# Taking VectorE's and GpSimd's SBUF-to-SBUF operations one at a time in the planner of a delta-rule and two-expert-layer kernel

## The chip, the cores and the metric

The kernel runs on one core of a Trainium2 chip. Its time is device microseconds of one execution; the figure for the kernel before is the median of three runs. A core has the engines TensorE (PE in the profile), VectorE (DVE), ScalarE (ACT) and GpSimd (POOL), each with its own in-order queue of instructions, and SyncE (SP), which here issues the DMA transfers.

## The reference

Three stages follow one another, all in float32. `q`, `k`, `v` are 4 x 8 x 768 x 48 (batch, heads, steps, head size):

```python
k_n = k / (np.linalg.norm(k, axis=-1, keepdims=True) + 1e-06)
for t in range(S):                       # S = 768
    y[:, :, t] = np.einsum('bhd,bhde->bhe', q[:, :, t], state)
    v_old = np.einsum('bhde,bhd->bhe', state, kt)
    state = state + bt * np.einsum('bhd,bhe->bhde', kt, vt - v_old)
...
# first expert layer, x is 3072 x 384, w_in 384 x 2048, w_out 2048 x 384
h = x @ w_in
P = a[0] + a[1] * h + a[2] * h2 + a[3] * h3
Q = 1.0 + np.abs(b[0]) * np.abs(h) + np.abs(b[1]) * h2
x = (P / (Q + 1e-06)) @ w_out
# second expert layer
r = np.maximum(x @ w_in, 0.0)
out = (r * r) @ w_out
```

## The kernel before

**Attention.** The 768 steps are cut into blocks; six groups, g = 0 to 5, each prepare 128 rows of small triangular systems. For a group a Gram matrix `Gb` (128 x 1024) is formed from `k`, scaled (L519 to L534), and a unit triangular matrix is inverted into `Tt` by 31 elimination steps of two instructions each: a product `tmp<-Gb,Tt` (L546) and a subtraction `Tt<-Tt,tmp` (L550), 128 x 31 up to 128 x 256 elements. Group 0's 62 instructions stand on VectorE, those of groups 1 to 5 on GpSimd. `vn` (128 x 768, the values by chunk) is scaled by L678. The products of the attention are PE's matmuls of L735; VectorE masks some of their results with `tri` (L780).

**Expert layers.** The 3072 tokens are six tiles of 512 columns (i = 0 to 5); the 2048 hidden features are sixteen blocks of 128 (j = 0 to 15). h(i,j) is the first product of a block, nine matmuls of L1031: weights `A` against the tile's high and low halves `xh` and `xl`. The rational function is a chain over PSUM and SBUF tiles: `a` (L1054), `b` (L1056 and L1066), `c` (L1058 to L1068), `h` and `g` (L1069 to L1071). Then `g` is cut in a high half `ph` (ScalarE, L1088) and a low half `pl` (GpSimd or VectorE, L1089), and acc(j), nine matmuls of L1118, adds the block to three accumulators from `ph`, `pl` and the weights `E` and `F` (L1115 with the unsplit weights `B` in the first tiles). Layer 2 has the same form with relu squared: `b`, `gh`, `gl` (L1132 to L1136) and L1145 to L1147 on weights `C`.

**Weights.** A block's input and output weights arrive packed, 128 x 768, in a staging buffer (`raw`, `rb`, `ra`, `mem`), are unpacked by ScalarE (L962) and VectorE (L964, L973 to L983), and are then split into halves: the high one by a ScalarE copy (L990, L997), the low one by a subtraction (L991 for `A`, L998 for `C`), on GpSimd or VectorE for `A` and on GpSimd for `C`. raw(l,j) is the load for layer l, block j. The loads of layer 2's first blocks alternate between two buffers `raw2_0` and `raw2_1`; a buffer can be loaded again when the `A` and the `C` split that read it are done. `rb0`, `rb1`, ... are further staging buffers.

**What sets the order.** All work is entered as tasks of a planner, class `Plan`: engine, planned duration, what is read and written, a due time. `play()` is a list scheduler: it holds a time at which each engine comes free, starts the task that can start first and, among those within 0.15 us, the one due first, and advances the engine by the planned duration. `run()` does eight rounds of it, moves the due times back from the uses in between, and keeps the best order. That order is then emitted, so that planned durations fix in which order instructions stand on each queue; on the chip each queue runs as data and semaphores allow. Tasks made by `shared` may go to GpSimd or VectorE, those made by `either` to ScalarE or VectorE; `play()` picks the engine. Each task carries a flag `lock`, set for operations whose operands lie in SBUF on VectorE and GpSimd, which `play()` does not read in the kernel before. A planned duration there is an average that includes some waiting, for example this one, with `SLOW` = 1.08:

```python
add(eng, (0.17 + 2.3e-3 * a * b) * (SLOW if g == 1 else 1) if g else 0.19 + 1.04e-3 * a * b, st, ...)
```

## Time and profile before

| | kernel before |
|---|---|
| median of 3 runs (lowest, highest) | 1009.11 us (1009.02, 1010.25) |
| the profiled execution's own time | 1008.75 us |
| its span, first to last instruction | 1007.0 us |
| PE busy | 958.9 us (95% of the span) |
| DVE, ACT, POOL busy | 686.4, 617.3, 510.0 us |
| mean granted TensorE clock | 0.97 |

The profiled execution lies 0.36 us under the median and has 1.75 us outside the span. A page shows busy time by engine; a table of windows shows it by stretch of the span; a list of waits names, for one engine, who it waited for; a timeline has the instructions of an engine in order of time with the idle time before each in brackets.

### The profile page before, as it was taken

The page shows a single profiled execution, that of the slowest core. Times are in us where ns is not written, and L with a number is a line of the kernel's source. Part 1 is how long each engine was busy: PE and PEld are TensorE (multiplying, and loading weights), DVE is VectorE, ACT ScalarE, POOL GpSimd, SP SyncE. Part 2 cuts the span into 40 slices and gives each one's busy share as a digit, 9 for nine tenths or more (in the row PEclk, how much of TensorE's full clock was granted, in tenths as well). Part 3 has the DMA queues.
Part 4 walks back from the last instruction along what each step waited for, and adds up shares of the span by engine and source line. Part 5 has one row for each costly group of instructions (what it writes and reads, how often), then busy time and mean ns, then how long its engine had stood idle before and what let it go on. Part 6 is the DMA issues. An engine that isn't in the chain of part 4 may idle for free.

```text
span 1007.0 us, 23528 instructions
## 1 busy us (share of the span) xinstructions
PE 958.9 (95%) x9611; PEld 770.5 (77%) x9611; DVE 686.4 (68%) x1100; ACT 617.3 (61%) x1121; POOL 510.0 (51%) x625
## 2 busy tenths in 40 slices
PE   5487999999999999999999999999999999999998
PEld 5485665688778878878888877888888888888886
DVE  6968988987987798789779999953343433434332
ACT  4668677888878697678779776743332333423322
POOL 3188998988998989875448986710000000000000
...
GB/s 160 253 223 128 142 212 206 83 54 131 64 109 96 140 89 43 84 109 46 34 68 63 36 122 261 115 53 11 1 63 1 32 32 0 32 1 1 32 1 31
DMA packets 126668, 84.66 MB, mean 84 GB/s; under 512 B 95584, under 2 KB 111520, under 8 KB 126560
## 3 DMA queue, kind: packets, MB, share of 16 engines
...
## 4 chain that ended last, share of the span: by engine, by line
PE 72%; POOL 15%; DVE 3%; ACT 3%; issue 3%; SPq 2%; DMA 1%; POOLq 0%; ACTq 0%; DVEq 0%
PE bank L1031 31%; PE bank L1118 11%; PE bank L735 7%; PE bank L1147 7%; PE bank L1145 7%; PE bank L1146 7%; POOL Tt L550 3%; POOL pl L1089 3%; POOL tmp L546 3%; POOL mem L1066 3%; SPq L357 2%; PE bank L638 1%; POOL A L991 1%; PE bank L1115 1%; PE bank L624 1%
## 5 line engine op out<-in xcount | busy, mean ns | idle before, releaser
L1031 PE MATMUL bank<-xh,A 128*128 128x512 f32 (+1 forms) x1170 | 301.5, 393 | 3.4 <-POOL A L991 3.1
L1031 PEld LDWEIGHTS bank<-xh,A 128*128 128x128 f32 x1170 | 217.6, 189 | 56.6 <-POOL A L991 6.7
L1133 DVE SCALAR_TENSOR_TENSOR mem<-bank,mem 128x512 f32<-128x512 f32 x96 | 66.2, 689 | 145.9 <-ACT mem L1132 145.9
L1031 PE MATMUL bank<-xl,A 128*128 128x512 f32 (+1 forms) x585 | 163.3, 388 | 0.0
L1132 ACT ACTIVATE mem<-bank 128x512 f32<-128x512 f32 x96 | 57.4, 598 | 147.3 <-PE bank L1031 145.5
L1066 POOL TENSOR_TENSOR mem<-mem 128x512 f32<-128x512 f32 x89 | 117.0, 1315 | 51.0 <-ACT mem L1058 46.7
L1031 PEld LDWEIGHTS bank<-xl,A 128*128 128x128 f32 x585 | 109.8, 189 | 22.6
L1089 POOL TENSOR_TENSOR pl<-mem,ph 128x512 fp32r<-128x512 f32 x80 | 106.4, 1330 | 22.4 <-ACT ph L1088 22.3
L1136 DVE TENSOR_TENSOR gl<-mem,gh 128x512 fp32r<-128x512 f32 x96 | 71.7, 747 | 63.3 <-ACT gh L1135 63.2
L1147 PE MATMUL bank<-gh,C 128*128 128x512 f32 x288 | 113.8, 395 | 0.0
L1145 PE MATMUL bank<-gl,C 128*128 128x512 f32 x288 | 113.6, 394 | 0.0
L1146 PE MATMUL bank<-gh,C 128*128 128x512 f32 x288 | 112.0, 389 | 0.0
L1135 ACT CAST gh<-mem 128x512 fp32r<-128x512 f32 x96 | 59.6, 621 | 78.2 <-DVE mem L1133 66.2
L1118 PE MATMUL bank<-pl,E 128*128 128x512 f32 x240 | 98.9, 412 | 6.9 <-POOL pl L1089 6.9
L550 POOL TENSOR_TENSOR Tt<-Tt,tmp 128x31 f32<-128x31 f32 (+15 forms) x155 | 93.0, 600 | 8.1
L1118 PE MATMUL bank<-ph,E 128*128 128x512 f32 x240 | 94.2, 393 | 0.0
L1118 PE MATMUL bank<-ph,F 128*128 128x512 f32 x240 | 94.2, 393 | 0.0
L546 POOL TENSOR_TENSOR tmp<-Gb,Tt 128x31 f32<-128x31 f32 (+15 forms) x155 | 86.8, 560 | 9.3
L1069 DVE SCALAR_TENSOR_TENSOR mem<-mem,par,bank 128x512 f32<-128x512 f32 x96 | 71.3, 743 | 29.4 <-ACT bank L1079 28.3
L1078 ACT ACTIVATE mem<-mem,par 128x512 f32<-128x512 f32 x96 | 69.4, 723 | 25.0 <-POOL mem L1066 23.6
L1054 ACT ACTIVATE mem<-bank 128x512 f32<-128x512 f32 x96 | 56.9, 593 | 42.3 <-PE bank L1031 32.7
L1067 DVE TENSOR_TENSOR mem<-bank,mem 128x512 f32<-128x512 f32 x96 | 65.7, 684 | 12.0 <-ACT mem L372 11.4
...
## 6 DMA issues: line engine op xcount, KB each, us to landing
raw<-in_w_dram SPq DMA_DIRECT2D x17, 768.0 KB, 4.8
rb<-in_w_dram SPq DMA_DIRECT2D x8, 768.0 KB, 5.0
...
```

The lines of the kernel that those rows point to most:

```text
L546: E_.tensor_tensor(tv, _mid(Gb[:, s, s + 1:32], [128, a, b]), Tt[:, 0:a, s:s + 1].to_broadcast([128, a, b]), op=ALU.mult)
L550: E_.tensor_tensor(Tt[:, 0:a, s + 1:32], Tt[:, 0:a, s + 1:32], tv, op=ALU.subtract)
L735: M.matmul(*y[:3], start=a, stop=z)
L1031: M.matmul(h, a, b, start=(m == 0), stop=(m == len(seq) - 1))
L1066: shared(1.32, 0.75, lambda E: E.tensor_tensor(b(), b(), a(), op=ALU.mult), r=[ak], w=[bk], due=due + 4.2)
L1069: q3 = lambda: V.scalar_tensor_tensor(c(), c(), s(0), h(), op0=ALU.add, op1=ALU.mult)
L1089: shared(1.3, 0.72, lambda E: E.tensor_tensor(slot[mk][0], g(), slot[pk][0], op=ALU.subtract), r=[gk, pk], w=[mk], due=due + 11.5, alloc=( ...
L1118: M.matmul(acc[d], a, b, start=(j == 0 and m == 0), stop=(j == NJ - 1 and m == 2))
L1136: add("DVE", 0.76, lambda: V.tensor_tensor(gl(), b(), gh(), op=ALU.subtract), r=[bk, gk, "late"], w=[lk], due=due + 5, lock=1, alloc=(("gl ...
L1145: M.matmul(acc[d], wh, gl, start=(j == 0), stop=False)
L1146: M.matmul(acc[d], wl, gh, start=False, stop=False)
L1147: M.matmul(acc[d], wh, gh, start=False, stop=(j == NJ - 1))
```

## The change

`play()` gets a second clock, `port`. A task with `lock` on VectorE or GpSimd may only start when `port` has passed, and sets it to its own end less 0.12 us, so that in the plan such operations of the two engines follow one another. The planned durations of these tasks become those that the operation has without another one beside it. `shared` gets an argument `free_port` that clears the flag; it is used for the scaling of `vn`. The tasks r1 and r2 lose the flag, the product `b` of the first blocks gains it. Nothing is computed in another way: what changes on the chip is the order of instructions on the queues, some buffers, and the engine of some alternates (five operations go from VectorE to GpSimd, among them a split of `A0` and layer 2's split of `A2`; two go from GpSimd to VectorE, one chunk of `vn` and pl(2,13)). Below L235 every line number of the changed kernel is 5 higher (L546 is L551, L550 is L555, L678 is L683, L991 is L996, L998 is L1003, L1031 is L1036, L1089 is L1094, L1118 is L1123).

```diff
-SLOW = 1.08
+PORT = ("DVE", "POOL")
...
             s = max(when[i], free_at[e])
+            if e in PORT and (t["alt"][e][2] if t["alt"] else t["lock"]):
+                s = max(s, port)
...
+        port = 0.0
         while True:
...
                 free_at[e] = end if e != "LAND" else 0.0
+                if e in PORT and t["lock"]:
+                    port = end - 0.12
...
-    def shared(dur, dve, f, **kw):
+    def shared(dur, dve, f, free_port=False, **kw):
 
-        return add(("POOL", "DVE"), (dur, dve), (lambda: f(P_), lambda: f(V)), lock=(1, 1), **kw)
+        return add(("POOL", "DVE"), (dur, dve), (lambda: f(P_), lambda: f(V)), lock=(0, 0) if free_port else (1, 1), **kw)
...
-                add(eng, (0.17 + 2.3e-3 * a * b) * (SLOW if g == 1 else 1) if g else 0.19 + 1.04e-3 * a * b, st, r=GB, w=[tt, tm_], due=d1, lock=1)
+                add(eng, 0.22 + 1.72e-3 * a * b if g else 0.19 + 1.04e-3 * a * b, st, r=GB, w=[tt, tm_], due=d1, lock=1)
...
-                    shared(1.55, 1.4, vs, r=[("nT", g % 2)], w=[("vn", cb, x) for x in range(B)], due=dn - 4)
+                    shared(1.5, 1.2, vs, free_port=True, r=[("nT", g % 2)], w=[("vn", cb, x) for x in range(B)], due=dn - 4)
...
-        shared(1.15, LOW, lambda E: E.tensor_tensor(Aw[j][:, so], af(), Aw[j][:, si], op=ALU.subtract),
+        shared(1.02, 0.54, lambda E: E.tensor_tensor(Aw[j][:, so], af(), Aw[j][:, si], op=ALU.subtract),
...
-            shared(1.32, 0.75, lambda E: E.tensor_tensor(b(), b(), a(), op=ALU.mult), r=[ak], w=[bk], due=due + 4.2)
+            shared(1.29, 0.7, lambda E: E.tensor_tensor(b(), b(), a(), op=ALU.mult), r=[ak], w=[bk], due=due + 4.2)
```

The other edits of the diff are of this last kind: a number for a planned duration (L973 1.05 to 0.95, L977 0.7 to 0.55, L979 0.84 to 0.66, L964 0.95 to 0.58, L983 1.15 to 0.95, L998 1.15 to 1.02, L1015 0.75 to 0.7, L1136 0.76 to 0.7).

**Place 1, GpSimd, end of group 1's elimination.** `Gb_129` and `Tt_131` are group 1's matrices, `Gb_128` and `Tt_130` group 2's; `A_88` is layer 1's split weight A4, which h(0,4) needs; `vn_144` and `vn_145` are two chunks of the values. Before, with the last elimination steps:

```order
L550 TENSOR_TENSOR Tt_131<-Tt_131,tmp_133 128x31
L991 TENSOR_TENSOR A_88<-B_179,A_88 128x384
L678 TENSOR_TENSOR vn_144<-vn_144,nT_140 128x768
L678 TENSOR_TENSOR vn_145<-vn_145,nT_140 128x768
L991 TENSOR_TENSOR A_89<-B_179,A_89 128x384
L546 TENSOR_TENSOR tmp_132<-Gb_128,Tt_130 128x31
```

After, some twenty rows earlier:

```order
L551 TENSOR_TENSOR tmp_133<-Gb_129,Tt_131 128x175
L683 TENSOR_TENSOR vn_145<-vn_145,nT_140 128x768
L555 TENSOR_TENSOR Tt_131<-Tt_131,tmp_133 128x25x7
L551 TENSOR_TENSOR tmp_133<-Gb_129,Tt_131 128x156
L555 TENSOR_TENSOR Tt_131<-Tt_131,tmp_133 128x26x6
```

and after, at the end of the elimination:

```order
L551 TENSOR_TENSOR tmp_133<-Gb_129,Tt_131 128x31
L555 TENSOR_TENSOR Tt_131<-Tt_131,tmp_133 128x31
L996 TENSOR_TENSOR A_88<-B_179,A_88 128x384
L996 TENSOR_TENSOR A_91<-ra_1079,A_91 128x384
L551 TENSOR_TENSOR tmp_132<-Gb_128,Tt_130 128x31
```

One chunk of `vn` now stands ahead of A4 and the other has left this queue; a split of A0 (`A_84<-mem,A_84`) also stands in the elimination now, some thirty rows ahead of A4.

**Place 2, VectorE and GpSimd, near the end of layer 1.** VectorE before, in the chain of block (5,12), whose tile is `bank4`; `raw2_0` holds layer 2's raw weights of blocks 1 and 3 in turn:

```order
L1067 TENSOR_TENSOR mem_102<-bank4_73,mem_102 128x512
L1068 SCALAR_TENSOR_TENSOR mem_102<-mem_102,par_82,bank4_73 128x512
L964 TENSOR_SCALAR raw2_0_7003<-raw2_0_7003 128x768
L991 TENSOR_TENSOR A2_86<-raw2_1_7004,A2_86 128x384
L1069 SCALAR_TENSOR_TENSOR mem_102<-mem_102,par_82,bank4_73 128x512
```

VectorE after, same chain, whose tile is now `bank3`:

```order
L1072 TENSOR_TENSOR mem_102<-bank3_72,mem_102 128x512
L1073 SCALAR_TENSOR_TENSOR mem_102<-mem_102,par_82,bank3_72 128x512
L988 SCALAR_TENSOR_TENSOR raw2_0_7003<-raw2_0_7003 128x768
L1074 SCALAR_TENSOR_TENSOR mem_102<-mem_102,par_82,bank3_72 128x512
L1075 SCALAR_TENSOR_TENSOR bank3_72<-mem_102,bank3_72 128x512
```

GpSimd before, from b(5,10) on; A1 and C1 are layer 2's splits of block 1:

```order
L1066 TENSOR_TENSOR mem_102<-mem_102 128x512
L991 TENSOR_TENSOR A1_85<-raw2_0_7003,A1_85 128x384
L1089 TENSOR_TENSOR pl1_2430<-mem_102,ph1_2428 128x512
L998 TENSOR_TENSOR C1_6982<-raw2_0_7003,C1_6982 128x384
L1056 TENSOR_SCALAR mem_102<-mem_102,par_82 128x512
```

GpSimd after, from pl(5,12) on, down to pl(5,15):

```order
L1094 TENSOR_TENSOR pl0_2441<-mem_102,ph0_2439 128x512
L996 TENSOR_TENSOR A1_85<-raw2_0_7003,A1_85 128x384
L1061 TENSOR_SCALAR mem_102<-mem_102,par_82 128x512
L1071 TENSOR_TENSOR mem_102<-mem_102 128x512
L1094 TENSOR_TENSOR pl1_2442<-mem_102,ph1_2440 128x512
L1094 TENSOR_TENSOR pl0_2441<-mem_102,ph0_2439 128x512
L1003 TENSOR_TENSOR C1_6982<-raw2_0_7003,C1_6982 128x384
L1094 TENSOR_TENSOR pl1_2442<-mem_102,ph1_2440 128x512
```

A1 and C1 moved from ahead of b(5,11) to behind pl(5,12) and pl(5,14); the split of A2 left VectorE's chain of block (5,12).

**Place 3, PE and GpSimd, start of layer 2.** PE before, from the end of acc(5,13) on; A2 with `xh`, `xl` is h(0,2) of layer 2, and the row behind it is the first of acc(5,14):

```order
L1118 MATMUL bank2_71<-ph1_2428,E3_3251 128x512
L1031 MATMUL bank3_72<-xh_100,A2_86 128x512 x6
L1031 MATMUL bank3_72<-xl_101,A2_86 128x512 x3
L1118 MATMUL bank0_69<-pl0_2429,E3_3251 128x512
L1118 MATMUL bank0_69<-ph0_2427,F3_3524 128x512
```

PE after, from the end of acc(5,15) on:

```order
L1123 MATMUL bank2_71<-ph1_2440,E3_3346 128x512
L1036 MATMUL bank5_74<-xh_100,A2_86 128x512 x6
L1036 MATMUL bank5_74<-xl_101,A2_86 128x512 x3
L1150 MATMUL bank0_69<-gl0_7000,C0_6981 128x512
L1151 MATMUL bank0_69<-gh0_6997,C0_6981 128x512
```

GpSimd before, from pl(5,15) on:

```order
L1089 TENSOR_TENSOR pl1_2430<-mem_102,ph1_2428 128x512
L991 TENSOR_TENSOR A3_87<-raw2_0_7003,A3_87 128x384
L991 TENSOR_TENSOR A4_88<-raw2_1_7004,A4_88 128x384
L998 TENSOR_TENSOR C3_6984<-raw2_0_7003,C3_6984 128x384
L991 TENSOR_TENSOR A5_89<-rb0_7457,A5_89 128x384
```

GpSimd after, from pl(5,15) on:

```order
L1094 TENSOR_TENSOR pl1_2442<-mem_102,ph1_2440 128x512
L996 TENSOR_TENSOR A2_86<-raw2_1_7004,A2_86 128x384
L1003 TENSOR_TENSOR C2_6983<-raw2_1_7004,C2_6983 128x384
L996 TENSOR_TENSOR A5_89<-rb0_7458,A5_89 128x384
L996 TENSOR_TENSOR A3_87<-raw2_0_7003,A3_87 128x384
L1003 TENSOR_TENSOR C3_6984<-raw2_0_7003,C3_6984 128x384
L996 TENSOR_TENSOR A6_90<-rb1_7584,A6_90 128x384
L1003 TENSOR_TENSOR C5_6986<-rb0_7458,C5_6986 128x384
L1003 TENSOR_TENSOR C6_6987<-rb1_7584,C6_6987 128x384
L996 TENSOR_TENSOR A7_91<-rb3_7711,A7_91 128x384
L1003 TENSOR_TENSOR C7_6988<-rb3_7711,C7_6988 128x384
L996 TENSOR_TENSOR A4_88<-raw2_1_7004,A4_88 128x384
```

h(0,2) moved from ahead of acc(5,14) to behind acc(5,15), and A4 is the eleventh split behind pl(5,15), where it was the second. On PE, h(0,4) (weights A4) stood behind acc(5,15), twelve matmuls of L1145 to L1147, and h(0,3); now it stands behind acc(5,15), h(0,2), h(0,3), and 33 matmuls of L1145 to L1147 (three whole blocks of nine and six more).

## Rows read from the trace of the kernel before

**Rows 1.** The page's busy times by engine.
```profile
PE 958.9 (95%) x9611; PEld 770.5 (77%) x9611; DVE 686.4 (68%) x1100; ACT 617.3 (61%) x1121; POOL 510.0 (51%) x625
```
**Rows 2.** Windows: stretch, its length, busy us (instructions) by engine, granted clock, DMA.
```profile
100.00:370.00 270.00, 261.72 (x3849) 196.90 (x3849) 229.85 (x376) 213.29 (x384) 241.07 (x315) 0.99 0.50 123
```
**Rows 3.** Waits of PE, whole span: us in total, times, longest.
```profile
PE bank L1118 <- POOL pl L1089: 6.9, 6, 2.4
PE bank L1031 <- POOL A L991: 3.1, 2, 2.1
```
**Rows 4.** Timeline of PE at three places: start, length, idle before in brackets.
```profile
99.94 2.03 PE L1031 MATMUL bank<-xh,A 128*128 128x512 f32 x6 [2.06 <-POOL A L991]
...
597.63 0.50 PE L1118 MATMUL bank<-pl,E 128*128 128x512 f32 x1 [1.81 <-POOL pl L1089]
...
606.10 1.52 PE L1031 MATMUL bank<-xh,A 128*128 128x512 f32 x6
...
608.14 0.48 PE L1118 MATMUL bank<-pl,E 128*128 128x512 f32 x1
```
**Rows 5.** Timeline of POOL behind group 1's elimination.
```profile
98.88 1.01 POOL L991 TENSOR_TENSOR A<-B,A 128x384 fp32r<-128x384 f32 x1
99.84 3.63 POOL L678 TENSOR_TENSOR vn<-vn,nT 128x768 f32<-128x768 f32 x2
```
**Rows 6.** Timeline of DVE ahead of group 1's scaling of Gb.
```profile
46.63 1.08 DVE L780 TENSOR_TENSOR X<-bank,tri 128x256 f32<-128x256 f32 x3
```
**Rows 7.** Groups of POOL in 49.8:99 (group 1's elimination): busy us, mean ns.
```profile
L550 POOL TENSOR_TENSOR Tt<-Tt,tmp 128x31 f32<-128x31 f32 (+15 forms) x31 | 19.8, 639 | 2.3
L546 POOL TENSOR_TENSOR tmp<-Gb,Tt 128x31 f32<-128x31 f32 (+15 forms) x31 | 18.8, 607 | 2.4
```
**Rows 8.** Groups of POOL in 283.6:357 (group 4's elimination).
```profile
L550 POOL TENSOR_TENSOR Tt<-Tt,tmp 128x31 f32<-128x31 f32 (+15 forms) x32 | 17.8, 556 | 1.6
L546 POOL TENSOR_TENSOR tmp<-Gb,Tt 128x31 f32<-128x31 f32 (+15 forms) x31 | 15.7, 508 | 1.7
```
**Rows 9.** Timeline of POOL, then of DVE, around 224.6: two operations side by side.
```profile
224.62 1.76 POOL L1089 TENSOR_TENSOR pl<-mem,ph 128x512 fp32r<-128x512 f32 x1 [0.43 <-ACT ph L1088]
...
224.69 0.55 DVE L1109 TENSOR_TENSOR F<-B,E 128x384 fp32r<-128x384 f32 x1
```
**Rows 10.** Groups of POOL in 100:370.
```profile
L550 POOL TENSOR_TENSOR Tt<-Tt,tmp 128x31 f32<-128x31 f32 (+15 forms) x94 | 56.5, 601 | 4.3
L1066 POOL TENSOR_TENSOR mem<-mem 128x512 f32<-128x512 f32 x42 | 55.2, 1314 | 12.5 <-ACT mem L1058 12.0 <-PE bank L1118 0.4
L546 POOL TENSOR_TENSOR tmp<-Gb,Tt 128x31 f32<-128x31 f32 (+15 forms) x95 | 51.4, 541 | 5.5
```
**Rows 11.** Timeline of POOL around the end of layer 1.
```profile
579.60 1.03 POOL L991 TENSOR_TENSOR A<-raw,A 128x384 fp32r<-128x384 f32 x1
...
582.58 1.03 POOL L998 TENSOR_TENSOR C<-raw,C 128x384 fp32r<-128x384 f32 x1
...
596.31 1.27 POOL L1089 TENSOR_TENSOR pl<-mem,ph 128x512 fp32r<-128x512 f32 x1 [0.68 <-ACT ph L1088]
...
606.76 1.30 POOL L1089 TENSOR_TENSOR pl<-mem,ph 128x512 fp32r<-128x512 f32 x1 [1.90 <-ACT ph L1088]
608.76 1.41 POOL L1089 TENSOR_TENSOR pl<-mem,ph 128x512 fp32r<-128x512 f32 x1 [0.69 <-ACT ph L1088]
614.28 2.83 POOL L991 TENSOR_TENSOR A<-raw,A 128x384 fp32r<-128x384 f32 x2 [4.11 <-ACT A L990]
...
625.71 2.78 POOL L998 TENSOR_TENSOR C<-rb,C 128x384 fp32r<-128x384 f32 x2
```
**Rows 12.** Timeline of DVE in the chain of block (5,12).
```profile
590.54 1.48 DVE L964 TENSOR_SCALAR raw<-raw 128x768 uint32<-128x768 uint32 x1
591.94 1.65 DVE L991 TENSOR_TENSOR A<-raw,A 128x384 fp32r<-128x384 f32 x1
```

**Rows 13.** The page's DMA issues: the raw loads, KB each, us from issue to landing.
```profile
raw<-in_w_dram SPq DMA_DIRECT2D x17, 768.0 KB, 4.8
```

32 lines of the change are left out of this document (16 added, 16 removed).

## The prediction

> **What bounds the kernel now.** I read the page's busy times first, then the windows, then the waits of PE, and last the timelines at the places which these name. The page shows PE busy for 958.9 of 1007.0 us [rows 1]: the same 9611 matmuls stay, so the change can only move the 48 us in which PE is not busy. The windows show where a helper is nearly as full as PE: in 100 to 370 us GpSimd is busy 241.07 of 270 us beside 261.72 of PE, so PE's idle time there is 8.3 us and GpSimd's 28.9 [rows 2]. The waits of PE say on whom that idle time depends: 6.9 us on `pl` of GpSimd in six waits, 3.1 us on the split `A` of GpSimd in two [rows 3]. Together these 10.0 us are what better order on GpSimd can give at most. The two largest single places that I could follow in the order are 2.06 us ahead of h(0,4) at 99.94 and 1.81 us ahead of acc(5,12) at 597.63 [rows 4]. GpSimd and VectorE do slow each other: the 62 elimination instructions of group 1 took 38.6 us [rows 7], the 63 of group 4 only 33.5 [rows 8]. A `pl` of 1.76 us stands beside a VectorE split of 0.55 us [rows 9], where one without neighbour took 1.27 [rows 11].
>
> **The change part by part.** The planned durations alone cost nothing on the chip, since no instruction is added or made shorter; what counts is the new order, in four terms.
>
> **First term, up to h(0,4).** PE's wait at 99.94 ends with A4's split on GpSimd, 98.88 plus 1.01, at 99.89 [rows 4, 5], behind the whole elimination of group 1. Three things change ahead of it. The three masks of L780, 1.08 us on VectorE ahead of the scaling of `Gb` [rows 6], move into group 0's elimination, so the scaling and GpSimd's chain may start earlier: between 0 and 1.1 us, and I take 0.4, since GpSimd has a clearing and a copy of its own to do ahead of its first step and the end of group 0's chain comes 1.1 us later. The split of A0 goes into the chain, 1.0 us by A4's own split [rows 5], and so does a chunk of `vn`, half of the pair's 3.63, 1.8 us [rows 5]. Against that, about 2.8 us of VectorE's operations with operands in SBUF leave the stretch (the A0 split, and three L964 that go to ScalarE, some 0.6 each by the plan's new numbers, which is no measurement; the one L964 shown took 1.48 [rows 12], which would make it 5). The pair of rows 9 says that 0.55 us of such work cost GpSimd 0.49 (1.76 less 1.27) [rows 9, 11], so 2.8 us are worth up to 2.5; I take 2.0. The bounds are 0 and the 5.1 us by which group 1's steps took longer than group 4's [rows 7, 8]. Sum: -0.4 + 1.0 + 1.8 - 2.0 = **+0.4 us**, between -2.06, where PE's wait is used up, and +2.8, where nothing is gained from the masks or the neighbours. VectorE's own order also changes there (two `c` products of the next block come ahead of the first block's `g`), so the first accumulation starts later; PE then reaches h(0,4) about a microsecond later than now, which A4 still covers.
>
> **Second term, 100 to 370.** GpSimd paces PE here, so I reckon its load. It loses both chunks of `vn`, 3.63 us [rows 5], and pl(2,13), 1.3 by the row at 596.31 [rows 11]. It gains three operations from VectorE: a split for the second layer-1 weights, 1.0 [rows 11], and two products `b` at 1.31 [rows 10], 3.6 together. Net -1.3. Beside that, the elimination steps here mean 601 and 541 ns [rows 10] against 556 and 508 in group 4 [rows 8]: 94 times 45 and 95 times 33 ns are 7.3 us which the neighbours cost over group 4's rate. The new plan keeps the two engines' operations apart, but only as long as the chip keeps the plan's times, because nothing on the chip makes one queue wait for the other. I take 0.8 of the 7.3. Sum: **-2.1 us**, between 0 and the 5.1 us of the waits left for this stretch (10.0 less 2.06 at 99.94, 1.81 at 597.63 and about 1 elsewhere) [rows 3, 4].
>
> **Third term, acc(5,12).** Its wait is 1.81 us [rows 4]. Back from it, the chain ran through the splits A1 and C1 on GpSimd, 1.03 each [rows 11], and through two VectorE operations in the middle of block (5,12), 1.48 and 1.65 [rows 12]. A1 and C1 now stand behind pl(5,12) and pl(5,14), and in place of the two VectorE operations stands one unpacking, which the plan has at 0.95 and for which I take the 1.48 of its neighbour at most. 2.06 us come off GpSimd and 1.65 or more off VectorE: the wait goes, **-1.8 us**, between 0 and -1.81. What is late next is pl(5,14): its cover, h(0,2) from 606.10 to 608.14 [rows 4], has moved behind acc(5,15), so PE comes to acc(5,14) at 606.10, or 604.3 with this gain, while pl(5,14) ended at 608.06 [rows 11]. It has to come 3.8 us sooner. By the chain (GpSimd's 2.06, VectorE's 1.65, and the next blocks' first steps that now stand ahead of the last steps of block (5,13)) I think that it does; the other case is a rival below.
>
> **Fourth term, h(0,4) of layer 2.** Count from the end of pl(5,14). PE then does seven blocks of nine matmuls (acc(5,14), acc(5,15), h(0,2), h(0,3) and three of layer 2) and six more matmuls; at 2.04 us a block (606.10 to 608.14) [rows 4] this is 15.6 us. A4 is the eleventh split behind pl(5,15), which ended 2.1 us after pl(5,14) (610.17 against 608.06) [rows 11]. At 1.03 us each [rows 11] A4 is ready after 13.4 us; at the mean of the ten splits from 614.28 to 628.49, 1.42 us [rows 11], after 17.7. Its load waits for C2, two splits behind pl(5,15), and lands 4.8 us later [rows 13], near 9.5; that leaves 3 to 7 us for the unpacking, so the queue and not the load should be last. PE waits 0 to 2.1 us; at the 1.76 of the slowed `pl` [rows 9] for every split it would be 5.9. I take **+1.5 us**, near the 1.42 that was measured for these very splits.
>
> The sum is +0.4 - 2.1 - 1.8 + 1.5 = -2.0 us. On the profiled run's 1008.75 (span 1007.0 and 1.75 around it) that gives 1006.75, and the median lies 0.36 over that run, so I forecast **1007.1 us** against 1009.11.
>
> [...] In rows 9 GpSimd's record starts first, at 224.62, and it is GpSimd that took 1.76 while VectorE's split, from 224.69, took its plain 0.55. [...]
>
> **The rivals.**
>
> *Deep gain.* Operations that the plan sets apart also stay apart on the chip. [...] For it speaks that all ten microseconds of rows 3 wait on operations that the new plan counts; against it rows 9, where the later starter won, and that nothing ties the two queues. PE's waits on GpSimd go, -10.0, and the splits at 1.03 leave no fourth term: 1009.1 - 10.0 = 999.1 us. [...]
>
> *Lost cover.* pl(5,14) does not come sooner than 608.06. PE then waits ahead of acc(5,14) with h(0,2) still to do: 2.0 us are added in place of the 1.8 gained, so 1007.1 + 3.8 = 1010.9. It decides as soon as pl(5,14) comes less than 2.0 us sooner. For it speaks ScalarE's `ph`, which GpSimd awaited for 1.90 and 0.69 us [rows 11].
>
> *More contention: the slower side.* The plan's durations are now shorter (a step of 256 elements 0.66 in place of 0.82 by the two formulas), so it packs GpSimd more tightly, while on the chip the steps still meet VectorE's. Once GpSimd lags behind the plan, each late `pl` or `A` is a wait of PE. If the neighbours give back nothing in group 1 (+2.8 in place of +0.4) and cost half as much again as the 7.3 us in 100 to 370 (-1.3 + 3.7 = +2.4 in place of -2.1), the sum is +4.9 and the time 1014.0. It turns the sign from some 4 us more than forecast. For it speaks that GpSimd has only 28.9 us idle there.
>
> *The plan moves, PE does not.* Waits change places and keep their sum: 1009.1.
>
> **How the numbers follow.** About 0.2%, 2 us, is what a measurement of this kernel can tell from no change, so same is 1007.1 to 1011.1. My forecast has 0.50, and its terms' bounds make its own range 1003.5 to 1010.5; its centre lies on the border, but the third term is the surest and the gains left in rows 3 are larger than what is taken, so 0.30 of it is faster, 0.20 same. The deep gain has 0.10, all faster. The lost cover has 0.13, 0.05 same and 0.08 slower with the fourth term's upper end on it. More contention has 0.17, slower; no movement 0.10, same. This gives faster 0.40, same 0.35, slower 0.25. The range from 1001.0 to 1013.5 leaves out the deep gain and about half of more contention, 0.19.
>
> **What would show it.** In the changed profile: A4 at 99.5 to 101 and PE's wait on it near 2 us (first term); waits of PE on `pl` and `A` in 100 to 370 summing to about 3 to 4 in place of 5 to 7 us (second); no wait ahead of acc(5,12), and none over 0.5 ahead of acc(5,14) (third); a wait on `A` of 0.5 to 2.5 us ahead of layer 2's h(0,4) (fourth). I am wrong if the elimination steps' mean moves by more than 40 ns either way, if pl(5,14) holds PE up, or if PE waits for VectorE in new places, which I priced at nothing outside the first term.

## The result, and the profile after

| | before | after |
|---|---|---|
| median, us (lowest to highest) | 1009.68 (1007.46 to 1012.64, 6 runs) | 1018.41 (1016.78 to 1019.88, 6 runs) |
| after by before | | 1.0086 (interval 1.0071 to 1.0100) |
| the profiled execution, us | 1008.75 | 1017.93 (span 1016.1) |

The change makes the kernel 8.7 us slower. The prediction of 1007.1 us was wrong, and the result lies outside its range of 1001.0 to 1013.5. The busy times of the page answer to [rows 1]:

```profile
PE 959.7 (94%) x9611; PEld 770.9 (76%) x9611; DVE 681.7 (67%) x1095; ACT 622.5 (61%) x1123; POOL 506.3 (50%) x628
```

PE's matmuls are the same and its busy time is 0.8 us more, ScalarE's 5.2 us more, and VectorE's and GpSimd's busy times even fell. Of the 9.1 us by which the span is longer, 8.3 are idle time of PE. To find where it arises, I laid PE's timelines side by side and noted when the same number of the expert layers' matmuls was done. The differences between two such marks, after less before, are a ledger of the loss:

| stretch (us, by the time of before) | what PE does at its end | difference, us |
|---|---|---|
| 0 to 121 | group 1, first blocks of layer 1 | -0.26 |
| 121 to 267 | groups 2 and 3 | -0.13 |
| 267 to 520 | groups 4 and 5 | **+2.96** |
| 520 to 606 | acc(5,13) | -1.75 |
| 606 to 612.6 | acc(5,15) and h(0,2) | +1.45 |
| 612.6 to 633 | the first blocks of layer 2 | **+6.81** |
| 633 to the end | | 0.00 |

The sum is +9.08. Three quarters of it arise within 20 us at the start of layer 2. The waits of PE name the places (us in total, times, longest); the first and the fourth line answer to [rows 3]:

```profile
PE bank L1123 <- POOL pl L1094: 7.4, 8, 2.5
PE bank L1120 <- DVE mem L1076: 5.7, 1, 5.7
PE bank L1150 <- DVE gl L1141: 4.6, 1, 4.6
PE bank L1036 <- POOL A L996: 0.3, 1, 0.3
PE bank L1123 <- DVE pl L1094: 1.3, 1, 1.3
```

The waits on GpSimd's `pl` have not shrunk (6.9 before), those on GpSimd's splits are down to 0.3 (3.1 before), the longest wait for VectorE's `mem` has grown from 1.7 to 5.7, and there are two new ones on VectorE, for `gl` and for `pl`. The third line is the place of the loss. PE's timeline there (start, length, idle before in brackets):

```profile
618.86 1.66 PE L1036 MATMUL bank<-xh,A 128*128 128x512 f32 x6
620.36 0.84 PE L1036 MATMUL bank<-xl,A 128*128 128x512 f32 x3
621.04 0.39 PE L1150 MATMUL bank<-gl,C 128*128 128x512 f32 x1
...
622.89 0.40 PE L1152 MATMUL bank<-gh,C 128*128 128x512 f32 x1
627.93 0.77 PE L1150 MATMUL bank<-gl,C 128*128 128x512 f32 x1 [4.64 <-DVE gl L1141]
...
630.63 2.44 PE L1036 MATMUL bank<-xh,A 128*128 128x512 f32 x6
```

PE does h(0,3), then the nine matmuls of acc(0,2), then waits 4.64 us for `gl` of h(0,3); it had itself ended h(0,3) only at 621.20. Behind the wait, matmuls take 0.63 to 0.77 us in place of 0.39. The windows (columns as in [rows 2]; PEclk is third from the end) show why:

```profile
625.00:629.00 4.00, 1.07 (x3) 0.91 (x4) 4.00 (x3) 1.78 (x3) 4.00 (x4) 0.59 0.89 307
629.00:632.50 3.50, 3.50 (x10) 2.73 (x9) 1.32 (x2) 0.54 (x1) 1.98 (x2) 0.50 0.99 386
632.50:636.00 3.50, 3.50 (x17) 2.87 (x16) 1.46 (x3) 2.05 (x4) 0.00 (x0) 0.99 0.39 157
```

The granted clock falls within the wait (0.59 over 625 to 629 us) and is 0.50 up to 632.5. The six matmuls and the first part of the next `h` take 2.70 + 2.28 us there, where the same work later in after, from 637.71 and from 633.60 on, takes 1.38 + 1.39 at a granted clock of 1.00: 2.2 us. With the wait that makes 6.8 us, the whole stage.

VectorE's timeline shows what stood ahead of that `gl`, and one line of ScalarE's the `gh` that it reads:

```profile
617.84 1.52 DVE L1141 TENSOR_TENSOR gl<-mem,gh 128x512 fp32r<-128x512 f32 x1
619.28 1.38 DVE L969 TENSOR_SCALAR rb<-rb 128x768 uint32<-128x768 uint32 x1
620.77 1.60 DVE L988 SCALAR_TENSOR_TENSOR rb<-rb 128x768 uint32<-128x768 uint32 x1
622.29 0.68 DVE L1138 SCALAR_TENSOR_TENSOR mem<-bank,mem 128x512 f32<-128x512 f32 x1
622.89 0.80 DVE L969 TENSOR_SCALAR raw<-raw 128x768 uint32<-128x768 uint32 x1
624.75 1.61 DVE L988 SCALAR_TENSOR_TENSOR raw<-raw 128x768 uint32<-128x768 uint32 x1 [1.05 <-ACT raw L967]
626.28 1.50 DVE L1141 TENSOR_TENSOR gl<-mem,gh 128x512 fp32r<-128x512 f32 x1
...
623.30 0.62 ACT L1140 CAST gh<-mem 128x512 fp32r<-128x512 f32 x1
```

The product L1138 of h(0,3) is done at 622.97, and `gh` at 623.92. `gl` could have followed then. But in VectorE's queue the two unpackings of raw(2,4) stand ahead of it, the second waits for ScalarE's piece L967, and `gl` ends at 627.78. Why raw(2,4) is unpacked so late is seen in SP's timeline: its loads wait for the buffers that A1, C1, A2 and C2 free. Those four splits the plan puts behind pl(5,12), pl(5,14) and pl(5,15). The loads of raw(2,3) and raw(2,4), first before, then after:

```profile
583.63 0.33 SPq L357 DMA_DIRECT2D raw<-in_w_dram  x1
604.89 0.33 SPq L357 DMA_DIRECT2D raw<-in_w_dram  x1
```

```profile
608.32 0.33 SPq L362 DMA_DIRECT2D raw<-in_w_dram  x1
613.78 0.36 SPq L362 DMA_DIRECT2D raw<-in_w_dram  x1
```

So the loads start 24.7 and 8.9 us later.

The chain alone doesn't explain the wait, though. Before, three unpackings stood in VectorE's queue among the steps to this `gl` as well, and from the end of h(0,3) to the end of its `gl` it took 6.1 us, against 6.6 after. The lines of before, the last of h(0,3), its `gl` and the first of acc(0,3):

```profile
616.94 0.86 PE L1031 MATMUL bank<-xl,A 128*128 128x512 f32 x3
...
622.34 1.52 DVE L1136 TENSOR_TENSOR gl<-mem,gh 128x512 fp32r<-128x512 f32 x1
...
625.19 0.40 PE L1145 MATMUL bank<-gl,C 128*128 128x512 f32 x1
```

What fell is PE's other work over that chain, its cover: before it was 7.4 us, from 617.80 to 625.19 (h(0,4), h(0,5) and fifteen matmuls of L1145 to L1147), and after 2.1 us, up to 623.29. The chain less the cover is 4.5 us, the wait. The late weights bear on the cover because with them h(0,2) and h(0,3) could hardly stand earlier in PE's order: GpSimd's split of A2 ended at 611.86 and h(0,2) began at 612.65, its split of A3 ended at 618.80 and h(0,3) began at 618.86.

### The profile page after: what moved, and what is told of

Read it like the earlier page. It is cut to its first block, busy times and chain, and to the rows that moved or that the text cites. A ratio compares the mean times of both kernels' runs of the same rounds, so it can differ in the third digit from the quotient of the medians.

```text
span 1016.1 us, 23496 instructions
## 1 busy us (share of the span) xinstructions
PE 959.7 (94%) x9611; PEld 770.9 (76%) x9611; DVE 681.7 (67%) x1095; ACT 622.5 (61%) x1123; POOL 506.3 (50%) x628
## 4 chain that ended last, share of the span: by engine, by line
PE 69%; POOL 16%; DVE 5%; ACT 5%; issue 3%; DMA 1%; SPq 0%; POOLq 0%; ACTq 0%; DVEq 0%
PE bank L1036 30%; PE bank L1123 9%; PE bank L1152 6%; PE bank L1150 6%; PE bank L740 6%; PE bank L1151 6%; POOL Tt L555 4%; POOL tmp L551 4%; PE bank L1120 3%; POOL mem L1071 3%; POOL pl L1094 3%; DMA kTg<-in_kS_dram 1%; ACT mem L1083 1%; DVE mem L1074 1%; ACT mem L1063 1%
## 5 line engine op out<-in xcount | busy, mean ns | idle before, releaser
L1036 PE MATMUL bank<-xh,A 128*128 128x512 f32 (+1 forms) x1170 | 302.1, 393 | 1.5 <-DVE mem L1076 1.1
L1036 PEld LDWEIGHTS bank<-xh,A 128*128 128x128 f32 x1170 | 216.8, 189 | 53.7 <-DVE mem L1076 2.4
L1138 DVE SCALAR_TENSOR_TENSOR mem<-bank,mem 128x512 f32<-128x512 f32 x96 | 66.3, 691 | 156.2 <-ACT mem L1137 156.1
L1036 PE MATMUL bank<-xl,A 128*128 128x512 f32 (+1 forms) x585 | 162.5, 386 | 0.0
L1071 POOL TENSOR_TENSOR mem<-mem 128x512 f32<-128x512 f32 x91 | 119.1, 1310 | 48.6 <-ACT mem L1063 46.5
L1036 PEld LDWEIGHTS bank<-xl,A 128*128 128x128 f32 x585 | 109.0, 188 | 22.6 <-DVE xl L1020 0.2
L1094 POOL TENSOR_TENSOR pl<-mem,ph 128x512 fp32r<-128x512 f32 x79 | 107.4, 1360 | 22.0 <-ACT ph L1093 18.3
L1123 PE MATMUL bank<-pl,E 128*128 128x512 f32 x240 | 98.6, 411 | 8.8 <-POOL pl L1094 7.4
L555 POOL TENSOR_TENSOR Tt<-Tt,tmp 128x31 f32<-128x31 f32 (+15 forms) x155 | 89.7, 579 | 9.6
L1123 PE MATMUL bank<-ph,F 128*128 128x512 f32 x240 | 94.3, 393 | 0.0
L1123 PE MATMUL bank<-ph,E 128*128 128x512 f32 x240 | 94.1, 392 | 0.0
L551 POOL TENSOR_TENSOR tmp<-Gb,Tt 128x31 f32<-128x31 f32 (+15 forms) x155 | 87.6, 565 | 8.7
L1072 DVE TENSOR_TENSOR mem<-bank,mem 128x512 f32<-128x512 f32 x96 | 65.9, 686 | 15.4 <-ACT mem L377 13.4
```

The source lines that it names most:

```text
L551: E_.tensor_tensor(tv, _mid(Gb[:, s, s + 1:32], [128, a, b]), Tt[:, 0:a, s:s + 1].to_broadcast([128, a, b]), op=ALU.mult)
L555: E_.tensor_tensor(Tt[:, 0:a, s + 1:32], Tt[:, 0:a, s + 1:32], tv, op=ALU.subtract)
L1036: M.matmul(h, a, b, start=(m == 0), stop=(m == len(seq) - 1))
L1071: shared(1.29, 0.7, lambda E: E.tensor_tensor(b(), b(), a(), op=ALU.mult), r=[ak], w=[bk], due=due + 4.2)
L1094: shared(1.3, 0.7, lambda E: E.tensor_tensor(slot[mk][0], g(), slot[pk][0], op=ALU.subtract), r=[gk, pk], w=[mk], due=due + 11.5, alloc=(( ...
L1123: M.matmul(acc[d], a, b, start=(j == 0 and m == 0), stop=(j == NJ - 1 and m == 2))
```

## The experiments

All but v2, e1 and e2 take the two plans' orders as tables, every task's engine and place in its queue, and mix them: each keeps all of one plan but for what its diff names. The numbers in the diffs are tasks. In the table are the medians and their ratio to before on the same chip (interval in brackets), and the ledger of each profiled execution, as differences from before in us. How well a stage repeats is seen from kernels that have after's order in it: 520 to 606 gives -1.74 to -1.79 in five of them, 606 to 612.6 gives +1.43 to +1.46, the last +5.97 to +6.81, 267 to 520 gives +1.35 to +2.96, and the first two vary by several us, so that nothing small is read from those. Behind 633 us only w1 (+0.52) and e1 (+1.20) lose more.

| kernel | median | ratio | 0–121 | 121–267 | 267–520 | 520–606 | 606–612.6 | 612.6–633 |
|---|---|---|---|---|---|---|---|---|
| after | 1018.41 | 1.0086 | -0.26 | -0.13 | +2.96 | -1.75 | +1.45 | +6.81 |
| h1_head_after | 1014.32 | 1.0053 (1.0030 to 1.0075) | +1.82 | -0.10 | +2.77 | +0.92 | 0.00 | 0.00 |
| h2_tail_after | 1017.95 | 1.0081 (1.0061 to 1.0101) | -0.31 | -0.06 | -0.54 | -0.33 | +1.45 | +6.19 |
| v1_weights_back | 1020.75 | 1.0109 (1.0085 to 1.0133) | +3.44 | +2.94 | +1.60 | +1.08 | +0.48 | +5.06 |
| v2_no_reads | 1018.65 | 1.0082 (1.0051 to 1.0114) | +3.07 | +2.09 | +2.67 | -1.76 | +0.91 | +3.92 |
| w1_pe_order | 1018.33 | one run | -0.88 | -0.05 | -0.33 | -0.03 | +3.54 | +6.77 |
| x2_gl_first | 1019.12 | one run | +2.16 | +0.73 | +1.35 | -1.79 | +1.46 | +6.30 |
| w2_two_alternates | 1022.09 | one run | +1.25 | -0.01 | +6.03 | -1.74 | +1.43 | +6.17 |
| w5_gb_copy_later | 1022.77 | one run | +1.41 | +3.33 | +3.31 | -1.76 | +1.43 | +5.97 |
| e1_port_only | 1030.94 | 1.0225 (1.0208 to 1.0243) | +15.10 | -2.29 | +8.95 | -1.67 | +0.76 | -0.41 |
| e2_durations_only | 1018.21 | 1.0093 (1.0080 to 1.0106) | +9.49 | -1.07 | -2.16 | +2.27 | +1.12 | +0.06 |
| best_four_moves | 1007.44 | 0.9979 (0.9969 to 0.9989) | -2.14 | -0.03 | +0.34 | -0.66 | -0.20 | -0.03 |
| best2_seven_moves | 1014.68 | 1.0054 (1.0041 to 1.0067) | +1.58 | -0.04 | +2.14 | +2.22 | -0.20 | -0.02 |

### Which half of the plan: h1 and h2

Task 2855 is h(5,4); from it on h1 has before's order, and h2 after's.

```
h1:  late = set(before[before.index(2855):])
     order = [i for i in after if i not in late] + [i for i in before if i in late]
h2:  tail = set(after[after.index(2855):])
     late = set(after) - tail
     order = [i for i in before if i in late] + [i for i in after if i in tail]
```

> All queues have the changed order up to h(5,4) (tile 5, block 4, some 527 us into the span), and the order of before from there. In the changed trace PE is 2.6 us behind the trace of before at that point and 9.1 us behind from layer 2's block 7 on. If the loss is made at the start of layer 2 (order of its weight work, or contention there), this kernel is about 2.6 us over before: 1012 us, and PE has no wait for gl over 1 us in layer 2. If the changed order of the earlier stages costs the time in a way that only shows later, it stays near 1018.

> The mirror: the order of before up to h(5,4), the changed one from there. If the loss is made at the start of layer 2: about 6.5 us over before, 1016 us, with a wait of PE for gl of 3 to 5 us near 625. If it comes out of the earlier stages: within 2 us of before.

Measured: h1 has 0.00 in both last stages, h2 +1.45 and +6.19, as after has. So the two last stages depend on the tail's order, and 267 to 520 us on the head's (+2.77 in h1, -0.54 in h2), by one profile each. The medians don't add up: h1 lies 4.8 us over before (1014.32 against 1009.51, forecast 1012), h2 8.4 us (1017.95, forecast 1016), the whole change 8.7. h2's profiled execution, 1015.14 us, is the fastest of its four and 2.8 us under their median, so its ledger shows less than a usual one. The sum of the halves comes near the whole only at the lower ends of their intervals; why, no run here shows. In h1's window of the last stages the granted clock is 1.00:

```profile
600.00:640.00 40.00, 38.24 (x164) 30.13 (x163) 37.82 (x47) 29.58 (x53) 27.89 (x22) 1.00 0.70 241
```

### What makes gl late: v1, v2, w1, x2

Four candidates: the late weights themselves, the contention of VectorE and GpSimd, PE's new order, and VectorE's order. v1 gives the layer-2 weight tasks of blocks 1 to 5 back before's engine and place, under after's order of PE:

```
late = set(range(3074, 3114))
order, eng = weave(T, after, before, ea, eb, late)
```

> The changed order throughout, but the tasks of layer 2's weights of blocks 1 to 5 (load, unpacking, splits) stand on their queues where before has them (A1 and C1 ahead of b(5,11), A2's split on VectorE in block (5,12)). Theory 'late load': C1's and C2's places set when the two staging buffers come free, so raw(2,3) and raw(2,4) are loaded 25 and 9 us later than before and their unpacking stands ahead of gl on VectorE; then this kernel loses that wait: no wait for gl over 1.5 us, 1018.4 less 6.5, plus 1 to 1.5 us for the wait ahead of acc(5,12) which comes back: 1013 us. Theory 'contention only' (VectorE's and GpSimd's operations there slow each other, wherever they stand): the wait stays at 3 to 5 us and the time at 1017 to 1019.

Measured: the wait for `gl` is still there, 2.5 us at most, and the stage costs +5.06. So the late load by itself is not the cause (that theory forecast 1013 us, and 1020.75 were measured), nor does the wait reach the 3 to 5 us forecast from contention alone. The waits of PE in 600 to 660 us:

```profile
PE bank L1208 <- DVE gl L1199: 3.0, 2, 2.5
```

v2 takes most of GpSimd's reads away in after, and so leaves out the low halves of the weights of layer 2's blocks 1 to 8:

```
+if E is P_ and l == 2 and 1 <= j <= 8:
+    E.memset(dst.bitcast(F32), 0.0)
+    E.tensor_copy(dst[:, 0:1], src[:, 0:1])
+else:
     E.tensor_tensor(dst, src, high, op=ALU.subtract)
```

> The changed order throughout; GpSimd's low splits of layer 2's blocks 1 to 8 are replaced by a clearing of the low half and a copy of its first column, so GpSimd reads next to nothing there (the output lacks the low halves of these weights). VectorE's instructions from 609 to 628 us took 7.3 us longer than their kind does elsewhere. Theory 'contention': they fall to 0.55 (L969), 0.95 (L988) and 0.69 us (gl), the wait of 4.6 us shrinks to under 1, the time to about 1012. Theory 'late load' alone: raw(2,4) still comes only after C2, the wait stays over 3 us, the time at 1016 to 1018. If it takes both together, this kernel and the one with the weights put back each lose the wait.

Measured: VectorE's timeline has its plain durations back, 0.96 for L988 (1.61 in after) and 0.69 for `gl` (1.50), and yet `gl` of h(0,3) waits, now for ScalarE's piece of raw(2,4). The first line is an earlier `gl`:

```profile
622.14 0.69 DVE L1147 TENSOR_TENSOR gl<-mem,gh 128x512 fp32r<-128x512 f32 x1 [0.30 <-ACT gh L1146]
...
628.62 0.96 DVE L988 SCALAR_TENSOR_TENSOR raw<-raw 128x768 uint32<-128x768 uint32 x1 [1.00 <-ACT raw L967]
629.49 0.69 DVE L1147 TENSOR_TENSOR gl<-mem,gh 128x512 fp32r<-128x512 f32 x1
```

PE waits 2.52 us and the stage costs +3.92. What v2 took away, contention and the longer splits on GpSimd together, is thus worth 2.9 of the 6.81 us in this one profile. That is no bound on the contention: an L969 that stands beside a clearing (622.82 to 623.24), at 622.75, still takes 0.90 us, where the one at 627.06 takes 0.55. The `gl` at 622.14, on the other hand, took its plain 0.69 while GpSimd cleared a tile from 622.08 to 622.50.

w1 gives before nothing but 18 PE tasks at after's places, all of them around the start of layer 2:

```
moved = {3040, 3041, 3232, 3233, 3235, 3243, 3056, 3217, 3218, 3059, 3219, 3251, 3062,
         3224, 3225, 3226, 3227, 3039}
order, eng = weave(T, before, after, eb, ea, moved)
```

> The order of before on every queue but PE's; PE has the changed order at the start of layer 2 (h(0,2) behind acc(5,15), h(0,4) to h(0,6) behind the first three blocks and more of layer 2's second product). In the changed order only the second product of block 2, nine matmuls or 2.05 us, lies between h(0,3) and acc(0,3), which needs gl(0,3): one ScalarE, one VectorE, one ScalarE and one VectorE instruction of 0.6 to 0.7 us each, 2.6 us and their hand-overs. Theory 'PE order': that alone makes PE wait for gl, 1 to 3 us, and lose 2 to 5 us with the lower clock that followed the wait of 2.5 us in the kernel with the weights put back. Theory 'late load and unpacking' alone: PE's order costs under 1 us here, since the weights come as before. Both: some 1.5 us more ahead of acc(5,14), whose cover h(0,2) is gone.

Measured: +3.54 and +6.77, with three waits of PE in 600 to 660 us where before had none of these. The last is the lost cover of `pl`, the first the one on `gl`:

```profile
PE bank L1209 <- DVE gl L1200: 3.1, 2, 2.9
PE bank L1209 <- ACT mem L436: 2.0, 1, 2.0
PE bank L1182 <- POOL pl L1153: 1.8, 1, 1.8
```

PE's order by itself, with early weights, makes PE wait for `gl`: h(0,3) has the same 2.1 us of cover as in after, its chain takes 4.9 us, and the wait is 2.92. With the 1.7 us that the matmuls behind it lose at a granted clock of 0.50 (628.8 to 632.2) this is 4.6 of the 6.77 us. The other two, the wait of 1.98 us at 616.82, are a third thing: PE waits there for ScalarE's copies of the accumulators, which before's ScalarE queue has behind h(0,2)'s work; after has no such wait. So the lost cover is worth 4.6 of the 6.8 us that after loses, and the longer chain, 6.6 in place of 4.9 us, the rest. (The +3.54 of 606 to 612.6 is the wait of 1.80 and 1.7 us lost at a granted clock of 0.50.) The converse, after's late places for the weights of blocks 3 and 4 under before's order of PE, was not tried: the queues then wait for each other in a circle. Another order of PE with A1 and C1 late is in e1 below.

x2 puts gl(0,3) (task 3231) ahead of the unpacking of raw(2,4) (3100) in after:

```
order = ahead(T, after, eng, [(3231, 3100)])
```

> The changed order with one move: on VectorE gl(0,3) stands ahead of the two unpacking instructions of raw(2,4). In the changed trace gl(0,3) ran at 626.28, its last input gh was there at 623.92, and PE needed it at 623.29. Theory 'PE order and queue': the wait for gl falls from 4.64 to about 2.2 us (its other half is the cover that PE's order does not give), the lower clock behind it lasts 3.4 us in place of 6.8, and the stretch loses 3 to 4.5 us against before in place of 6.8. Theory 'late weights': the unpacking of raw(2,4), now 1.5 us later, is itself what PE needs next: PE then waits 2 to 3 us for A4 ahead of h(0,4), and the stretch still loses 6 to 7 us.

Measured: the wait for `gl` falls to 1.57 us, and the next `h` then waits 3.03 for A4:

```profile
626.51 0.50 PE L1199 MATMUL bank<-gl,C 128*128 128x512 f32 x1 [1.57 <-DVE gl L1190]
...
631.20 2.93 PE L1085 MATMUL bank<-xh,A 128*128 128x512 f32 x6 [3.03 <-POOL A L1045]
```

The stage stays at +6.30, within the spread of after's order. Two walls stand close behind each other, and the late weights are the second: in after A4's split ran from 627.20 to 628.67 and was hidden behind the wait for `gl` and the matmuls after it.

### The loss in 267 to 520: w2 and w5

In after the first waits of the stretch on `pl` are 1.51 us at 277.49, 2.55 at 284.42 and, for pl(2,13), which has moved from GpSimd to VectorE, 1.34 at 362.49. The elimination's groups in 100 to 370 us (busy us, mean ns, idle before) answer to [rows 10]:

```profile
L555 POOL TENSOR_TENSOR Tt<-Tt,tmp 128x31 f32<-128x31 f32 (+15 forms) x95 | 53.3, 561 | 5.6
L551 POOL TENSOR_TENSOR tmp<-Gb,Tt 128x31 f32<-128x31 f32 (+15 forms) x95 | 52.9, 556 | 4.9
```

One fell from 601 to 561, the other rose from 541 to 556, and GpSimd's load in the window fell:

```profile
100.00:370.00 270.00, 260.68 (x3971) 196.01 (x3970) 229.44 (x373) 214.74 (x383) 237.82 (x316) 0.99 0.52 124
```

3.25 us less than in [rows 2], and still PE waits more. w2 gives two operations, b(2,0) and pl(2,13), back to before's engine:

```
moved = {1589, 1819}
order, eng = weave(T, after, before, ea, eb, moved)
```

> The changed order throughout, but two operations have the engine and the place of before: the product b(2,0) is VectorE's again (the changed order has it on GpSimd right ahead of pl(1,15)), and pl(2,13) is GpSimd's again (the changed order has it on VectorE). Between the marks at 267 and 520 us of before, the changed trace lost 3.0 us. If it is these two places: the wait of 2.55 us near 284 falls to 1.0 to 1.5 and the one of 1.34 near 362 to under 0.3, and the stretch loses 0.5 or less against before. If it is GpSimd's load or contention in general: both waits stay and the stretch still loses 2.5 to 3 us.

Measured, in one run: +6.03, more than any kernel with after's own order there. The wait of 2.55 us near 284 did fall, to 0.93, but four waits for VectorE's `mem`, 3.2 us together, came in its place, and the wait for pl(2,13) is longer on GpSimd than on VectorE:

```profile
365.56 0.50 PE L1181 MATMUL bank<-pl,E 128*128 128x512 f32 x1 [2.75 <-POOL pl L1152]
```

So giving back the choice of engine at these two places does not undo the loss. w5 keeps after's engines and puts part of block (2,13)'s work ahead: one ScalarE piece of it (task 1814) ahead of the copy of `Gb` (1950), and VectorE's three operations on it ahead of c(2,14) (1828), which had stepped in front. It does less than its expectation says: a(2,14), b(2,14) and `ph` of (2,13) still stand behind the copy.

```
order = ahead(T, after, eng, [(1814, 1950), (1815, 1828), (1816, 1828), (1817, 1828)])
```

> The changed order throughout, but ScalarE's copy of Gb (2.1 us, at 355.7) stands behind h(2,13), a(2,14) and b(2,14) as before has it, and on VectorE the last three steps of block (2,13) stand ahead of the first two of block (2,14). Theory: the wait of 1.34 us near 362 (for pl(2,13)) comes from this copy, which the plan pulled forward because group 3's elimination ends earlier; then that wait falls under 0.3 and the stretch 322 to 520 us loses about 0.6 us against before in place of 2.0. Rival: pl(2,13) is late because VectorE makes it behind r1; then the wait stays.

Measured: +3.31, no gain, with the wait for pl(2,13) at 3.09 us, on VectorE:

```profile
367.89 0.50 PE L1172 MATMUL bank<-pl,E 128*128 128x512 f32 x1 [3.09 <-DVE pl L1143]
```

In w5's trace the copy runs at 360.03, and a(2,14) at 363.62 and `ph` of (2,13) at 365.69 follow it. The theory that the copy makes the wait is therefore not tested by w5. In after `ph` was there at 361.09, and in VectorE's queue three small operations of the elimination's head, 0.79, 0.35 and 0.19 us from 360.30 on, stand directly ahead of pl(2,13) at 361.66; they can hold it up by at most 0.6 of the 1.34 us. Which step of the new order costs the 1.4 to 3.0 us stays open.

### Either half of the planner's edit: e1 and e2

```
e1 (before, with the port only):          e2 (after, without the port):
+PORT = ("DVE", "POOL")                   -if e in PORT and (t["alt"][e][2] if t["alt"] else t["lock"]):
+if e in PORT and (... t["lock"]):        -    s = max(s, port)
+    s = max(s, port)
+port = end - 0.12
```

> The kernel before with the planner's port clock alone: all planned durations stay the old ones. Its order has A1 and C1 late as in the changed kernel, but on PE three h blocks and the second product alternate so that 1.3 to 2 blocks and one h lie between h(0,3) and acc(0,3). Theory 'PE order': no wait for gl over 1 us at the start of layer 2, and that stretch loses under 1.5 us against before; the rest of the kernel may move by 3 us either way: 1008 to 1013. Theory 'late load of the weights': that stretch loses 4 us or more as with the whole change: 1014 to 1020.

> The changed kernel without the port clock: the new planned durations alone. On PE each h of layer 2 stands 1.3 to 1.7 blocks ahead of its own accumulation, A1 and A2 stand earlier than in the changed kernel. Theory 'PE order': no wait for gl over 1 us at the start of layer 2. The elimination steps are planned shorter than they run beside VectorE, so GpSimd lags behind its plan and PE's waits for pl between 100 and 600 us grow over the 6.9 us of before, to 8 to 12: 1010 to 1015. If durations without a wait were harmless, the waits stay at 6 to 7 us and the time within 2 us of before.

Measured: both are slower, at 1.0225 and 1.0093 of before (1030.94 and 1018.21 us; forecast 1008 to 1013 and 1010 to 1015), and elsewhere than after is. e1 holds PE up for 15.15 us ahead of the first accumulations, e2 for 6.55 on a split:

```profile
109.29 5.49 PE L1121 MATMUL bank<-mem,B 128*128 128x512 f32 x6 [15.15 <-DVE mem L1077]
```

```profile
90.85 1.65 PE L1034 MATMUL bank<-xh,A 128*128 128x256 f32 x6 [6.55 <-POOL A L994]
```

Neither loses at the start of layer 2 (-0.41 and +0.06), although e1 has A1 and C1 late too; there PE's order keeps two `h` and more than a block between h(0,3) and acc(0,3), 6.7 us of cover (638.91 to 645.62) over a chain of 6.2 us, and PE doesn't wait for `gl`. A late A1 and C1 alone do not make the loss, then; it takes PE's order too.

### Moves by hand: best_four_moves and best2_seven_moves

Before's order, with the items of GpSimd for which PE waits put forward one by one: A4 ahead of group 2's first steps, pl(1,14) ahead of an elimination step, pl(1,0) ahead of b(1,2), and A2's split moved from VectorE to GpSimd, ahead of b(5,15).

```
best:   order = ahead(T, before, eng, [(279, 873), (1351, 1446), (1077, 1106), (3087, 3044)])
best2:  ... and (285, 519), (1368, 1451), (3081, 2970)
```

> The order of before with four moves on GpSimd's queue: the split A4, whose inputs are there at 82.3 and which ran at 98.9, ahead of the scaling of group 2's matrix (near 92); pl(1,14), ready at 273.1 and run at 276.1, two instructions earlier; pl(1,0) ahead of b(1,2); the split of A2 from VectorE's chain of block (5,12) to GpSimd behind pl(5,12). If PE's waits hang on what stands right ahead in one queue, the waits of 2.06, 2.35, 0.93 and 1.81 us each fall to under 0.5, the lower clock after 278 goes too (1.7 us), and the time is 5 to 8 us under before: 1001 to 1004. If GpSimd's load sets the pace there, the waits come back one or two blocks later and the time is within 2 us of before.

> The four moves of the kernel with four moves, and three more on GpSimd's queue: A5 ahead of the pair of vn, pl(1,15) some nine instructions earlier, C1 behind b(5,11). In the kernel with four moves the waits came back one block later: 1.52 us for A5 at 103.8, 3.21 for pl(1,15) at 281.2, and 1.32 of the wait for pl(5,12) was left. If each is again what stands right ahead: these three fall under 0.5 us, the lower clock behind 281 goes, and the time is 3 to 5 us under the kernel with four moves: 1002.5 to 1004.5. If GpSimd has no more slack, they come back once more and the time stays at 1006 to 1008.

Measured: best_four_moves beats both kernels, 1007.44 us and 0.9979 of before (0.9969 to 0.9989), 2.1 us. That is short of the 1001 to 1004 us forecast, and near the second reading, within 2 us of before. The wait of 2.06 ahead of h(0,4) is gone, but in its timeline the next ones stand in its place, on VectorE's `mem`, on A5 and on pl(1,15):

```profile
99.44 2.84 PE L1169 MATMUL bank<-mem,B 128*128 128x512 f32 x6 [1.45 <-DVE mem L1125]
...
103.80 1.67 PE L1085 MATMUL bank<-xh,A 128*128 128x512 f32 x6 [1.52 <-POOL A L1045]
...
281.22 0.50 PE L1172 MATMUL bank<-pl,E 128*128 128x512 f32 x1 [3.21 <-POOL pl L1143]
```

best2 moves A5 ahead of the pair of `vn`, pl(1,15) ahead of an elimination step, and C1 one `b` back as well, and is slower than before (1.0054; forecast 1002.5 to 1004.5 us, 1014.68 measured). Now pl(2,0) is late:

```profile
290.59 0.79 PE L1172 MATMUL bank<-pl,E 128*128 128x512 f32 x1 [4.05 <-POOL pl L1143]
```

Here, bringing one item forward in a full queue delayed the next: the waits moved on, and with seven moves they grew.

## Why the prediction was wrong, step by step

**The fourth term is the step that failed** (+1.5 forecast, bounded by 0 to 2.1, and 5.9 with every split slowed; +6.81 measured). It priced PE's wait for A4 alone and put PE's wait for `gl` of h(0,3) at nothing. It went wrong in two ways.

*It counted one chain.* I priced PE's wait for A4 alone, and treated the postponed A1, C1, A2 and C2 as relief for GpSimd (the third term). I did not follow what those four free: the buffers of raw(2,3) and raw(2,4), and so their loads, and so VectorE's and ScalarE's unpacking, which then stood in the middle of layer 2's first blocks, ahead of `gl` of h(0,3). That chain came first: a wait of 4.64 us for `gl`, plus 2.2 us at a granted clock of 0.50. The prediction quoted the order in which PE does h(0,3) three blocks ahead of h(0,4), yet did not ask how much work lies between h(0,3) and the accumulation that needs its `gl`. This is the larger part of the mistake: the cover fell from 7.4 us to nine matmuls, 2.1 us, while the chain of ScalarE, VectorE, ScalarE and VectorE went from 6.1 only to 6.6 us. The prediction's last sentence names "if PE waits for VectorE in new places, which I priced at nothing", and that is what happened. h1 and h2 place this loss in the tail's order; w1 shows that PE's order alone makes 4.6 us of it, v1 that early weights alone don't mend it, x2 that A4 is the next wall, v2 that contention and longer splits are worth some 2.9 us of it.

*The chain it did count was short by 4.5 us at its upper value.* I had A4 ready 13.4 to 17.7 us after pl(5,14). By GpSimd's timeline pl(5,14) ended at 606.46 and A4's split at 628.67, so 22.2 us. The ten splits ahead of it, from 610.38 on, took 14.2 us together, a mean of 1.42, exactly the value I took. Missing were 2.90 us in which GpSimd waited for A5's pieces, whose unpacking was late, and 1.9 us because pl(5,15) ended 4.0 us behind pl(5,14) and not 2.1. "The queue and not the load should be last" was half right. PE would have come to h(0,4) at 624.7 without the wait for `gl`, and waited some 4 us; x2 shows 3.03.

**The second term has the wrong sign** (-2.1 forecast; -0.13 measured in 121 to 267 us and +2.96 in 267 to 520, +1.35 at least in the other kernels with that order). Its reckoning of GpSimd's load held: forecast net -1.3 and 0.8 of the neighbours', measured -3.25 us busy. The step that failed is the sentence before it: that GpSimd paces PE in this stretch, so that load comes off PE's time. The load came off and PE's waits on `pl` and `A` in 100 to 370 us, forecast at 3 to 4, sum to 6.5 us, against 7.5 before. In the runs here single items that come late make the waits, and a new order made other items late. w2 speaks against one further reading of mine, w5 does not test the other, and the cause of this loss stays open.

**The first term came out near by luck** (+0.4 forecast, -0.26 measured at 121 us). Six other profiles of kernels with after's head lie at +1.25 to +3.44, two of them above the term's upper bound of 2.8, so that it was likely 1 to 2 us too small; and the mechanism was another. A4 ended at 102.12 instead of 99.89, 2.2 us later and beyond the 101 that I gave. PE nevertheless didn't wait for it, since the first accumulation had already waited 5.67 us for VectorE, and two blocks of accumulations then ran in a row:

```profile
94.73 8.06 PE L1120 MATMUL bank<-mem,B 128*128 128x512 f32 x12 [5.67 <-DVE mem L1076]
102.23 1.95 PE L1036 MATMUL bank<-xh,A 128*128 128x512 f32 x6
```

before waited 1.39, 1.71 and 2.06 us at three places there. "About a microsecond later" for that accumulation was too little. And the contention in group 1 didn't go down: over the group's 62 steps, from 48.2 to 101.2 us, the two kinds mean 631 and 628 ns, against 607 and 639 in [rows 7].

**The third term was right** (-1.8 forecast): the wait ahead of acc(5,12) went from 1.81 to 0.33 us, and the stage to acc(5,13) gained 1.75 us.

**The lost cover came, one block later.** pl(5,14) ended 1.6 us sooner than before (606.46 against 608.06), less than the 2.0 from which the prediction lets it decide, and still held nobody up, because PE had lost 2.6 us in the stages before and came to acc(5,14) only at 606.92. pl(5,15) did: PE came to it at 609.13, about 1.1 us earlier than before, while it started at 608.63, nearly as before (608.76), since it waited for ScalarE's `ph`, and took 1.79 us beside VectorE's unpacking and a `gl`, where before it took 1.41 [rows 11]. With h(0,2) now behind acc(5,15) nothing covered it:

```profile
608.63 1.79 POOL L1094 TENSOR_TENSOR pl<-mem,ph 128x512 fp32r<-128x512 f32 x1 [0.34 <-ACT ph L1093]
```

```profile
610.48 0.50 PE L1123 MATMUL bank<-pl,E 128*128 128x512 f32 x1 [1.35 <-POOL pl L1094]
```

The stage lost 1.45 us, of 3.8 that the rival had.

**The other rivals.** The deep gain fell: the operations did not stay apart, as the 609 to 628 us show (GpSimd's split from 617.05 to 618.80 beside VectorE's `gl` from 617.84 to 619.36). More contention had the right sign and the wrong place: what v2 took away is worth 2.9 us, and that at the start of layer 2, not in group 1 and 100 to 370. What the prediction read from [rows 9], that the later starter won, rests on two records whose starts lie 0.07 us apart, which is thin for saying who came first. The range was too narrow, because every term had bounds but a chain that no term named had none.
